# Attention, MoE and soft-MoE in one kernel: an earlier reciprocal and earlier turns of q and k in the first attention; masks, evictions and the scaling of q moved between engines in chunk 1

## The chip, the cores and the metric

The kernel runs on one core of a Trainium2 chip. The metric is device time in microseconds, lower is better. A core has TensorE (PE for its matmuls, PEld for its weight loads), VectorE (DVE), ScalarE (ACT), GpSimd (POOL) and SyncE (SP, which issues the transfers here). Each works through its own list of instructions in order, and semaphores tie the lists together.

## The reference

Three stages follow each other. `setup_inputs` scales q and k by 8 and phi by 200 and gives every input as float64; the kernel reads q, k, v and the weights as they are handed over.

```python
# 1: attention, q, k, v of shape (4, 8, 576, 64); heads 0-3 plain window 32, heads 4-7 dilated by 4
scores = scale * np.matmul(q, k.transpose(0, 1, 3, 2))
mask_plain = (rel >= 0) & (rel < window)
mask_dil = (rel >= 0) & (rel < window * dilation) & (rel % dilation == 0)
scores = np.where(masks[None, :, :, :], scores, -1000000000.0)
attn = np.exp(scores - np.max(scores, axis=-1, keepdims=True))
attn = attn / (np.sum(attn, axis=-1, keepdims=True) + 1e-09)
x = np.matmul(attn, v)                       # then (2304, 512)
# 2: h = x @ w_in (512 x 2048); x = (h - tanh(h)) @ w_out (2048 x 512)
# 3: logits = x @ phi (512 x 32); soft mixture over 8 experts of 512 -> 1024 -> 512, 4 slots each
d = np.exp(logits - logits.max(0)); d /= d.sum(0) + 1e-9; slot_input = d.T @ x
slot_out[e] = np.maximum(slot_input[e] @ w1[e], 0.0) @ w2[e]
c = np.exp(logits - logits.max(1)); c /= c.sum(1) + 1e-9; out = c @ slot_out
```

## The kernel before, in words

The 2304 tokens are worked in four chunks of 512 (one batch each) and a rest of 256. While the tokens of one chunk go through `w_in`, the attention of the next batch is computed between the matmuls. Batch 0 has nothing to run beside, so its attention stands at the front (the first attention); then comes chunk 0 of the matmuls, `mixed_step` s = 0 to 7, with the attention of batch 1 in it (the change's words call that attention "chunk 1", by its batch; this text says the mixed chunk for the eight steps). `phase_step` does the later chunks, and the experts end the kernel.

**One unit of attention.** A batch has four pairs of heads, taken in the order `PO = (2, 3, 0, 1)`, and twelve units, three for each pair. A unit goes through: `emit_scores` (8 or 6 small matmul groups on PE into a PSUM tile `mm`, L359), a row maximum on DVE (L374), exponentials on ACT (L377), a reciprocal of the sums on DVE (L391), a multiplication by it on POOL (L392), transposes on PE (L401), their eviction by ACT (`ENGS['pt']`, L103), products with v on PE (L422), and evictions of the result as a rounded high part by ACT (`xhi`) and a low part by DVE (`xlo`, L458). For batch 0 the mask is added by one more matmul (L337: a bf16 identity times a bf16 mask opens the sum in PSUM, `by_pe`), for the others DVE adds it (L371) and the exponentials read the SBUF copy.

**q and k.** For batch 0, `emit_qk` turns k (n = 0) and q (n = 1) of a pair by PE transposes (L308); k is evicted by DVE (L103), q by ACT with the factor 0.125 (L316). For later batches POOL scales q (`scale_q`, L250) and DVE turns both in blocks (`turn_qk`, L260 and L261).

**The weights.** They arrive as 64-bit words and are put together as float32: `conv_a` on ACT (L507, the high word), `conv_b` on DVE (a shift of a word, L515, and a shift with an or, L516: the word shifts). For `w_in`, `conv_in_c` casts a high part (`wh`, L103) and subtracts a low part on POOL (L529). For `w_out`, `conv_out_c` transposes the block on PE (L537) and evicts the turned words by the engine in `ENGS['wt'][ft % 2]`, so before by ACT for even blocks and by DVE for odd ones; `conv_out_d` writes the block back to DRAM and multiplies by phi on PE (L548).

**What sets the order.** In the front every step is put on a list by `at(t, ...)` with a nominal time, and the list is sorted; the times order the instructions of every engine and do nothing else. The units have `ATT0 = (8.71, 3.45)` (start and pitch); in pitches after its start a unit has its reciprocal at `NORM`, transposes at `TRANS`, products with v at `PV`; q and k of the next pair come at `QK`; blocks of `w_in` begin at `WI`, with `conv_b` at `CB` and `conv_in_c` at `IC` pitches after. `warm` fills PE with matmuls whose result is not used (L205). `mixed_step` and `phase_step` are written out in order. SP's queue follows the same program: each transfer waits there for its buffer, in order. PSUM has five `mm` buffers in turn and two `h` buffers.

**One mixed step s.** It has the h matmuls of blocks 2s and 2s + 1 (12 each: L574, L575, L576), tanh on ACT (L580), a subtraction on DVE (L583), `conv_a` to `conv_in_c` of the `w_in` blocks 2s + 2 and 2s + 3, `conv_out_c` to `conv_out_d` of the `w_out` blocks 2s + 4 and 2s + 5, `conv_a` and `conv_b` of the next two, scores of two units (2s, 2s + 1), transposes and v products of the two units before, and at s = 0, 1, 2, 4 (`QKS`) a `turn_qk`.

Of the kernel before, what the change touches and what calls it, by code (L numbers as in the profile page):

```python
# [13 lines left out]
ACTF = mybir.ActivationFunctionType  # L14
ALU = mybir.AluOpType
# [13 lines left out]
UNITS = 16  # L29
KA = 6  # L30
CAL = 2.29
MASKPE = 1
PO = (2, 3, 0, 1)
VB = (1, 2, 3)
EA = (1,)
# [1 line left out]
    ("out", 0): 0, ("out", 2): 1, ("out", 4): 2, ("in", 0): 3, ("in", 2): 0, ("in", 4): 1, ("out", 6): 2, ("in", 6): 3,  # L37
    ("out", 8): 2, ("out", 10): 1, ("in", 8): 2, ("in", 10): 3, ("out", 14): 2, ("in", 14): 3,
}
ENGS = {'qk': 'VVAA', 'pt': 'AAA', 'hi': 'AAA', 'rem': 'VVA', 'wh': 'VA', 'wt': 'AV', 'wq': 'V', 'wp': 'A'}  # L40
WARM = 5
NWARM = 4
WAT = 0.29
ATT0 = (8.71, 3.45)
NORM = (1.01, 0.28)
TRANS = [2.05] * 10 + [1.9, 1.3]
PV = [3.15] * 9 + [2.95, 2.5, 1.9]
QK = (1.54, 1.08)
LQK = (12.33, 21.85)
LV = (4.31, 7.03)  # L50
DT0 = 5.58
# [3 lines left out]
CB = 0.96  # L55
OC = 1.64
OD = 3.09
OE = 3.85
WI = (45.0, 4.0)
LWI = 2.97  # L60
IC = 0.34

# [2 lines left out]
def moe_kernel(ctx: ExitStack, tc: tile.TileContext, q, k, v, w_in, w_out, phi, w1, w2, out):  # L65
    nc = tc.nc
# [34 lines left out]
    def copy(eng, out, in_):  # L101

        (nc.scalar.copy if eng == "A" else nc.vector.tensor_copy)(out=out, in_=in_)  # L103
# [10 lines left out]
    def cpart(*dims):  # L114
        o = moff[0]
        moff[0] += size(dims)
        return view(mem[:, o:o + size(dims)], dims)
# [38 lines left out]
    wp = cpart(NFT, NS)  # L156
# [90 lines left out]

    def scale_q(b, p):
        t = raws[b, p]
        nc.gpsimd.tensor_scalar(out=t[:, 0], in0=t[:, 0], scalar1=0.125, scalar2=None, op0=ALU.mult)  # L250

    def turn_qk(b, p):

# [34 lines left out]
    def emit_qk(b, p, n):  # L288
# [16 lines left out]
        for th in range(2):  # L305
# [4 lines left out]
            if p >= NP // 2:  # L310
                ps = ps.rearrange("p e (h x) -> p e h x", h=2)
            eng = ENGS["qk"][2 * n + th]
            if n == 0:
# [12 lines left out]
    def emit_scores(b, *units):  # L326

        work = []
        for i in units:
# [3 lines left out]
            mask = mask_d[:, (0, 4, 2)[u]:(4, 8, 6)[u]] if nb == 4 else mask_p[:, min(u, 1):min(u, 1) + 3]  # L333
            by_pe = b < MASKPE
            nr = nq if by_pe else 64
# [59 lines left out]
    def emit_trans(b, i):  # L395
# [6 lines left out]
        pt = pts.next()[0:nk, 0:nb * P].rearrange("p (c k) -> p c k", c=nb)  # L402
        copy(ENGS["pt"][min(b, 2)], pt, ps)
        sc_pt[b, i] = pt

    def emit_pv(b, i):
# [44 lines left out]
        for src, f in pieces:  # L451
            copy(ENGS["hi"][min(b, 2)], f(hi), src)

        def low():
            for src, dst in rems:
                copy(ENGS["rem"][min(b, 2)], dst, src)
            for src, f in pieces:
# [62 lines left out]
    def win(part, ft):  # L520
        return wts[ft // 2][:, part, :, 128 * (ft % 2):128 * (ft % 2) + 128]

    def conv_in_c(ft):
# [3 lines left out]
        hi, lo = win(0, ft), win(1, ft)  # L527
        copy(ENGS["wh"][ft > 1], hi, fv)
        nc.gpsimd.tensor_tensor(out=lo, in0=fv, in1=hi.bitcast(F32), op=ALU.subtract)  # L529
# [3 lines left out]
    def conv_out_c(ft):  # L533
# [4 lines left out]
        wt = convs["wt"].next()  # L538
        copy(ENGS["wt"][ft % 2], wt, ps)
        wstate["wt", ft] = wt  # L540
# [26 lines left out]
    def emit_h(xh, xl, ft, ps=None, part=range(KT)):  # L567

        if ps is None:
            ps = ps_h.tile([128, 512], F32, tag="h", name="h")[:, 0:xh.shape[-1]]  # L570
        for n in part:
            kt = PO[n]
            wh, wl = win(0, ft)[:, kt, :], win(1, ft)[:, kt, :]
            nc.tensor.matmul(ps, lhsT=wh, rhs=xh[:, kt, :], start=(n == 0), stop=False)  # L574
            nc.tensor.matmul(ps, lhsT=wh, rhs=xl[:, kt, :], start=False, stop=False)  # L575
            nc.tensor.matmul(ps, lhsT=wl, rhs=xh[:, kt, :], start=False, stop=(n == KT - 1))  # L576
        return ps
# [301 lines left out]
    with tc.manual_schedule():  # L879
# [4 lines left out]
        def at(t, f, *args):  # L884
            steps.append((t, len(steps), f, args))

        for b, (t0, dt) in enumerate((ATT0,)):
            for i in range(NU):
                t = t0 + dt * i
                at(t - 0.01, emit_lows)  # L890
                at(t, emit_scores, b, i)
                at(t + NORM[b] * dt, emit_norm, b, i)
                at(t + TRANS[i] * dt, emit_trans, b, i)
                at(t + PV[i] * dt, emit_pv, b, i)
                if b == 0:
                    at(t + WAT * dt, warm, WARM if i < NWARM else 2)
            for i in (NU, NU + 0.55, NU + 0.95):
                at(t0 + dt * i, emit_lows)
            for p in range(NP):
                for n in range(2):  # L900
                    at(t0 - 0.02 + 0.01 * n if p == 0 else t0 + dt * (3 * p - 3 + n + QK[b]), emit_qk, b, PO[p], n)
                at(t0 + dt * 3 * p - LQK[b], load_qk, b, PO[p])
                at(t0 + dt * 3 * p - LV[b], load_v, b, PO[p], nc.sync)
# [4 lines left out]
        for e in range(KA):  # L908
            t, dt = WO1[0] + WO1[1] * e, WO1[1]
# [6 lines left out]
        for e in range(4):  # L916
            t, dt = WI[0] + WI[1] * e, WI[1]
            at(t - LWI if e < 2 else 45.0, load_w, "in", e)
            at(t, conv_a, "in", e)
            at(t + CB, conv_b, "in", e)  # L920
            at(t + IC * dt, conv_in_c, e)
        first = []
        for i in range(2):

            at(ATT0[0] + ATT0[1] * (12.6 + 0.4 * i), lambda i: first.append(emit_h(xhi[0], xlo[0], i, part=range(3))), i)
        at(WI[0] + 6.0, scale_q, 1, PO[0])
        for _, _, f, args in sorted(steps, key=lambda s: s[0:2]):
            f(*args)
        emit_lows()
# [14 lines left out]
        def mixed_step(an, ch, s, xh, xl, gs, posts):  # L944
# [47 lines left out]
            if s + 1 in QKS:  # L992
                scale_q(an.b, PO[QKS.index(s + 1)])
# [4 lines left out]
        def phase_step(an, ch, s, xh, xl, gs, posts):  # L998
# [29 lines left out]
            if an and s + 1 in QKS:  # L1028
                scale_q(an.b, PO[QKS.index(s + 1)])
# [133 lines left out]
        for a, copy in enumerate((nc.scalar.copy, nc.vector.tensor_copy)):  # L1163
            ps = mm([128, 2, 32])
            for c in range(2):
                dt = 2 * a + c
# [32 lines left out]
        for cols in halves:  # L1199
# [4 lines left out]
                out=sS[64:96, cols], in0=ps[64:96], in1=sS[64:96, cols].bitcast(F32), op=ALU.subtract  # L1204
# [49 lines left out]
```

## Time and profile before

| | |
|---|---|
| median of three runs (lowest to highest) | 460.63 us (460.35 to 463.51) |
| the profiled execution | 460.01 us, span 458.2 us |
| mean granted TensorE clock | 0.973 of full |
| busy share of the span | PE 92%, PEld 67%, DVE 58%, ACT 44%, POOL 18% |

The profile's shares are averages over stages that have different limits. The first attention ends at about 61 us, the mixed chunk runs to about 146 us, and from there on PE is nearly always busy. A wait of an engine is told with what released it: `[2.32 <-DVE qk L261]` reads as 2.32 us of idle time which DVE's line 261 ended. [...]

### The profile page before, as it was taken

How to read it: one execution, taken by the hardware profiler on the slowest of the kernel's cores; microseconds unless marked ns; L12 is line 12 of the kernel's file. 1: busy time of each engine (PE TensorE's matmuls, PEld its weight loads, DVE VectorE, ACT ScalarE, POOL GpSimd, SP SyncE). 2: the span in 40 equal slices, each digit the busy share in tenths (PEclk: the TensorE clock that was granted, in tenths of full speed). 3: DMA queues.
4: the chain of work that ended last, by engine and by line, in shares of the span. 5: the costliest groups of instructions: out<-in, count | busy, mean ns of one | idle time of the engine just before them, and what ended most of it. 6: DMA issues, size and time to landing. Idle time of an engine off the chain costs nothing.

```text
span 458.2 us, 11352 instructions
## 1 busy us (share of the span) xinstructions
PE 420.3 (92%) x4555; PEld 306.5 (67%) x4555; DVE 264.6 (58%) x625; ACT 200.1 (44%) x693; POOL 83.5 (18%) x99
## 2 busy tenths in 40 slices
PE   6988688898999999999999999999999999999980
PEld 4766466666777776877775777776777689555330
DVE  2666549979897667765576777444544331332051
ACT  3766438667577173655153564331211223213141
POOL 3231423424224231313031211000000000010000
PEclk9999789899899999999999999999999999999996
DMA  8999974879667303243503212094003599899938
GB/s 242 238 222 280 281 127 145 268 149 277 229 177 127 75 1 54 61 69 54 121 20 54 41 40 94 1 362 191 0 1 109 186 407 409 313 405 408 408 121 313
DMA packets 102021, 81.16 MB, mean 177 GB/s; under 512 B 78032, under 2 KB 81872, under 8 KB 101968
## 3 DMA queue, kind: packets, MB, share of 16 engines
q1 hardware_dynamic: 101968, 80.43, 58.2%
q8 instruction: 36, 0.59, 0.6%
q14 instruction: 17, 0.14, 0.1%
HBM read 71.50 MB, written 8.91 MB: 175 GB/s over the span
## 4 chain that ended last, share of the span: by engine, by line
PE 68%; DVE 14%; ACT 7%; DMA 4%; issue 2%; SPq 2%; POOL 1%; DVEq 0%; POOLq 0%; ACTq 0%
PE h L574 12%; PE h L576 11%; PE h L575 11%; PE mm L713 4%; PE lg L589 4%; ACT mem L377 3%; PE mm L359 3%; PE h L797 3%; PE mm L422 3%; PE y L822 3%; PE mm L401 3%; PE warm L205 2%; SPq L243 2%; DMA wo<-wo_dram 1%; DVE cva L516 1%
## 5 line engine op out<-in xcount | busy, mean ns | idle before, releaser
L574 PE MATMUL h<-xhi,wts 128*128 128x512 f32 x256 | 107.0, 418 | 0.0
L576 PE MATMUL h<-xhi,wts 128*128 128x512 f32 x256 | 101.4, 396 | 0.5 <-POOL wts L529 0.5
L575 PE MATMUL h<-xlo,wts 128*128 128x512 f32 x256 | 101.6, 397 | 0.0
L580 ACT ACTIVATE mem<-h 128x512 f32<-128x512 f32 x72 | 43.0, 599 | 120.1 <-PE h L576 112.6
L583 DVE TENSOR_TENSOR mem<-h,mem 128x512 f32<-128x512 f32 x72 | 49.0, 681 | 68.5 <-ACT mem L580 68.5
L392 POOL TENSOR_TENSOR mem<-mem 128x320 f32<-128x320 f32 (+1 forms) x48 | 32.9, 695 | 156.2 <-DVE mem L391 92.9
L574 PEld LDWEIGHTS h<-xhi,wts 128*128 128x128 f32 x256 | 49.4, 193 | 15.9 <-issue 5.5
L576 PEld LDWEIGHTS h<-xhi,wts 128*128 128x128 f32 x256 | 48.9, 191 | 12.1 <-POOL wts L529 0.9
L575 PEld LDWEIGHTS h<-xlo,wts 128*128 128x128 f32 x256 | 49.2, 192 | 8.8
L377 ACT ACTIVATE mem<-mem 128x80 f32<-128x80 f32 (+1 forms) x126 | 44.5, 355 | 17.0 <-DVE mem L374 17.0
L596 DVE STREAM_TRANSPOSE gt<-mem 128x512 f32<-128x512 f32 x64 | 40.9, 681 | 0.0
L103 ACT COPY mem<-mm 80x448 f32<-80x448 f32 (+4 forms) x64 | 25.5, 430 | 9.0 <-PE mm L401 7.8
L359 PE MATMUL mm<-qk 64*64 64x96 f32 (+2 forms) x672 | 23.5, 246 | 5.0 <-ACT qk L316 2.6
L422 PE MATMUL mm<-mem,v 80*64 80x48 f32 (+1 forms) x672 | 26.8, 229 | 1.0 <-ACT mem L103 1.0
L401 PE MATMUL mm<-mem 112*80 112x112 f32 (+1 forms) x168 | 23.8, 275 | 4.2 <-POOL mem L392 4.2
L589 PE MATMUL lg<-mem 128*32 128x128 f32 x576 | 25.9, 279 | 0.9 <-DVE mem L583 0.9
L422 PEld LDWEIGHTS mm<-mem,v 80*64 80x64 f32 (+1 forms) x672 | 22.8, 140 | 5.5 <-ACT mem L103 1.7
L359 PEld LDWEIGHTS mm<-qk 64*64 64x64 f32 (+1 forms) x672 | 18.0, 133 | 10.9 <-issue 4.7
L377 ACT ACTIVATION_READ_ACCUMULATOR mem<-mem 128x1 f32 x126 | 23.6, 187 | 0.0
L401 PEld LDWEIGHTS mm<-mem 112*80 112x80 f32 (+1 forms) x168 | 16.6, 124 | 9.6 <-POOL mem L392 5.5
L589 PEld LDWEIGHTS lg<-mem 128*32 128x32 f32 x576 | 14.9, 109 | 11.6 <-issue 9.0
L377 ACT ACTIVATE mem<-mm,mem 128x80 f32<-128x80 f32 (+1 forms) x42 | 13.5, 331 | 15.6 <-DVE mem L389 9.6
(178 smaller groups left out, 634.2 us busy)
## 6 DMA issues: line engine op xcount, KB each, us to landing
ex<-in_moe_w_dram SPq DMA_DIRECT2D x21, 1024.0 KB, 10.7
gt<-in_moe_w_out_dram SPq DMA_DIRECT2D x7, 1024.0 KB, 8.1
gt<-in_moe_w_in_dram SPq DMA_DIRECT2D x7, 1024.0 KB, 8.3
gt<-in_moe_w_dram SPq DMA_DIRECT2D x6, 1024.0 KB, 9.8
mem<-in_moe_w_dram SPq DMA_DIRECT2D x5, 1024.0 KB, 7.1
wo_dram<-cva SPq DMA_DIRECT2D x16, 256.0 KB, 6.0
wo<-wo_dram SPq DMA_DIRECT2D x4, 1024.0 KB, 7.5
out_dram<-o SPq DMA_DIRECT2D x8, 512.0 KB, 4.8
```

The costliest lines, as they stand in the source:

```text
L359: nc.tensor.matmul(ps[64 * y:64 * y + nr, c, :], lhsT=qT[b, p][r, q0:q0 + step * (nr - 1) + 1:step], rhs=kT[b, p][r, k0:k0 + step * (nk - ...
L377: nc.scalar.activation(out=pr[:, c, :], in_=ps[:, c, :], func=ACTF.Exp, bias=nm[:, c:c + 1], accum_out=sm[:, c:c + 1],)
L392: nc.gpsimd.tensor_tensor(out=pr, in0=pr, in1=rc.unsqueeze(2).to_broadcast([128, nb, nk]), op=ALU.mult)
L401: nc.tensor.transpose(ps[:, c, :], pr[0:P, c, :], ident[0:P, 0:P])
L422: nc.tensor.matmul(o[64 * hh:64 * hh + 64, col:col + nq], lhsT=vt[b, p](n, hh), rhs=pt[:, c, 64 * (x ^ sw):64 * (x ^ sw) + nq], start=True ...
L574: nc.tensor.matmul(ps, lhsT=wh, rhs=xh[:, kt, :], start=(n == 0), stop=False)
L575: nc.tensor.matmul(ps, lhsT=wh, rhs=xl[:, kt, :], start=False, stop=False)
L576: nc.tensor.matmul(ps, lhsT=wl, rhs=xh[:, kt, :], start=False, stop=(n == KT - 1))
L580: nc.scalar.activation(out=g, in_=ps, func=ACTF.Tanh)
L583: nc.vector.tensor_tensor(out=g, in0=ps, in1=g, op=ALU.subtract)
L589: nc.tensor.matmul(lgs[ch][32 * j:32 * j + 32, 0:128], lhsT=wp[:, ft, :], rhs=g[:, 128 * j:128 * j + 128], start=(ft == 0), stop=(ft == NF ...
L596: nc.vector.transpose(out=gt[:, ft, :], in_=g)
```

## The change

It changes numbers that order the front, two settings that choose an engine, and one function.

- `NORM`: the reciprocal of the last unit of the first attention stands at 0.6 of a pitch in place of 1.01; `WI`, and the times of `conv_b` and `conv_in_c` of the first four `w_in` blocks, are set anew.
- `QK` for batch 0: 0.75 in place of 1.54, so k and q of a pair are turned one unit sooner.
- `MASKPE = 2`: the masks of batch 1 are added by PE too (12 more matmuls), and the 12 additions on DVE go.
- `ENGS['wt'] = 'AA'`: turned words of odd `w_out` blocks are evicted by ACT as well (three in the first attention, five in the mixed chunk).
- `scale_q`: ACT scales q of batch 1, in place of POOL; the first of these stands at 56.0 on the list in place of 51.0.

```diff
-MASKPE = 1
+MASKPE = 2
-ENGS = {'qk': 'VVAA', 'pt': 'AAA', 'hi': 'AAA', 'rem': 'VVA', 'wh': 'VA', 'wt': 'AV', 'wq': 'V', 'wp': 'A'}
+ENGS = {'qk': 'VVAA', 'pt': 'AAA', 'hi': 'AAA', 'rem': 'VVA', 'wh': 'VA', 'wt': 'AA', 'wq': 'V', 'wp': 'A'}
-NORM = (1.01, 0.28)
+NORM = [1.01] * 11 + [0.6]
-QK = (1.54, 1.08)
+QK = (0.75, 1.08)
-WI = (45.0, 4.0)
+WI = (43.5, 4.0)
     def scale_q(b, p):
         t = raws[b, p]
-        nc.gpsimd.tensor_scalar(out=t[:, 0], in0=t[:, 0], scalar1=0.125, scalar2=None, op0=ALU.mult)
+        if b in EA:
+            nc.scalar.activation(out=t[:, 0], in_=t[:, 0], func=ACTF.Copy, scale=0.125)
+        else:
+            nc.gpsimd.tensor_scalar(out=t[:, 0], in0=t[:, 0], scalar1=0.125, scalar2=None, op0=ALU.mult)
...
-                at(t + NORM[b] * dt, emit_norm, b, i)
+                at(t + NORM[i] * dt, emit_norm, b, i)
...
             at(t, conv_a, "in", e)
-            at(t + CB, conv_b, "in", e)
-            at(t + IC * dt, conv_in_c, e)
+            at(t + 3.3, conv_b, "in", e)
+            at(t + (5.4 if e < 2 else 3.4), conv_in_c, e)
...
-        at(WI[0] + 6.0, scale_q, 1, PO[0])
+        at(56.0, scale_q, 1, PO[0])
```

The new lines in `scale_q` move what follows down by three lines: L359 before is L362 in the changed kernel.

DVE at the end of the first attention, before, from the maximum of unit 10 to the reciprocal of unit 10. L374 is a unit's maximum, L389 and L391 its reciprocal, L515 and L516 the word shifts (`cvb` is `w_in` block 0, `mem` block 1):

```order
L374 TENSOR_REDUCE mem<-mm 128x3
L389 TENSOR_SCALAR mem<-mem 128x3
L391 RECIPROCAL mem<-mem 128x3
L515 TENSOR_SCALAR cvb<-cvb 128x512
L516 SCALAR_TENSOR_TENSOR cvb<-gt,cvb 128x512
L103 CAST wts<-cvb 128x4x128
L103 COPY mem<-mm 128x16
L458 TENSOR_TENSOR xlo<-mm,xhi 128x3x48
L458 TENSOR_TENSOR xlo<-mm,xhi 128x32
L374 TENSOR_REDUCE mem<-mm 128x3
L389 TENSOR_SCALAR mem<-mem 128x3
L391 RECIPROCAL mem<-mem 128x3
```

The second L374 is that of unit 11, which thus stands behind the word shifts and the cast of block 0. Six rows further on (two copies, the word shifts of block 1 and the subtractions, L458) DVE comes to the last reciprocal, that of unit 11. The same stretch in the changed kernel, from the maximum of unit 11:

```order
L377 TENSOR_REDUCE mem<-mm 128x3
L392 TENSOR_SCALAR mem<-mem 128x3
L394 RECIPROCAL mem<-mem 128x3
L518 TENSOR_SCALAR cvb<-cvb 128x512
L519 SCALAR_TENSOR_TENSOR cvb<-gt,cvb 128x512
L103 COPY cvb<-mm 128x128
L392 TENSOR_SCALAR mem<-mem 128x3
L394 RECIPROCAL mem<-mem 128x3
L103 CAST wts<-cvb 128x4x128
```

The maximum of unit 11 and the reciprocal of unit 10 now stand ahead of the word shifts of block 0, and the last reciprocal ahead of those of block 1 and of the cast.

PE in the first attention, before, around the scores of unit 3, the first of the second pair. L308 turns q of that pair, L359 are the scores that need it:

```order
L205 MATMUL warm<-mem 128x256
L308 MATMUL mm<-mem,rqk 128x96 x6
L337 LDWEIGHTS mem
L337 MATMUL mm<-mem 128x320
L359 MATMUL mm<-qk 48x80 x8
L401 MATMUL mm<-mem 80x112 x4
```

In the changed kernel the same turn (L311) stands ahead of the scores of unit 2, and a whole unit with its warm-up lies between it and the scores of unit 3:

```order
L205 MATMUL warm<-mem 128x256
L311 MATMUL mm<-mem,rqk 128x96 x6
L340 LDWEIGHTS mem
L340 MATMUL mm<-mem 128x320
L362 MATMUL mm<-qk 48x80 x8
L404 MATMUL mm<-mem 80x112 x4
```

Both turns of each of the three later pairs move by one unit like that.

ACT in mixed step 1 of the changed kernel. L583 is the tanh of an h block, L510 `conv_a`, L380 the exponentials, `cvb<-mm 128x512` the evictions of turned words:

```order
L583 ACTIVATE mem<-h 128x512
L510 ACTIVATE cvb<-gt 128x512
L510 ACTIVATE mem<-gt 128x512
L103 COPY cvb<-mm 128x512 x2
L583 ACTIVATE mem<-h 128x512
L103 COPY mem<-mm 80x448 x2
L103 CAST wts<-cvb 128x4x128
L103 CAST wts<-mem 128x4x128
L510 ACTIVATE cva<-gt 128x512 x2
L380 ACTIVATE mem<-mm,mem 128x80 x4
L385 ACTIVATE mem<-mem 128x4
L251 ACTIVATE rqk<-rqk 128x576
```

Before, the list had one eviction there, exponentials that read SBUF (`mem<-mem`), and no scaling (L251) at its end. SP's list is the same in both kernels.

## Rows read from the trace of the kernel before

**Rows 1.** Windows: length, busy us (count) PE, PEld, DVE, ACT, POOL, PEclk, DMA, GB/s.

```profile
51.50:61.20 9.70, 8.61 (x48) 7.03 (x49) 3.52 (x13) 3.06 (x9) 3.54 (x3) 0.50 0.83 218
70.30:144.20 73.90, 66.80 (x728) 52.38 (x725) 67.06 (x143) 51.48 (x175) 25.74 (x25) 0.95 0.71 201
108.40:123.80 15.40, 13.12 (x134) 10.33 (x131) 14.01 (x29) 8.90 (x29) 5.95 (x6) 0.89 0.85 252
123.80:134.90 11.10, 10.22 (x120) 7.88 (x118) 10.66 (x26) 8.80 (x29) 3.50 (x5) 1.00 0.50 157
```

**Rows 2.** Waits of PE, 8 to 48 us: total us, times, longest us.

```profile
PE mm L359 <- ACT qk L316: 2.6, 3, 1.4
```

**Rows 3.** Timeline, 40 to 70 us: start, us, engine, line, operation [idle before <- releaser].

```profile
43.67 0.53 PE L401 MATMUL mm<-mem 128*96 128x128 f32 x3
51.51 0.88 PE L401 MATMUL mm<-mem 128*96 128x128 f32 x3 [3.10 <-POOL mem L392]
55.35 0.87 PE L401 MATMUL mm<-mem 128*96 128x128 f32 x3 [1.08 <-POOL mem L392]
...
69.53 0.82 PE L359 MATMUL mm<-qk 64*64 64x80 f32 x32 [2.32 <-DVE qk L261]
```

**Rows 4.** Timeline of PE and of DVE, first attention: a mask matmul, a maximum from PSUM.

```profile
10.23 0.31 PE L337 MATMUL mm<-mem 64*128 64x320 bf16 x1
...
8.25 0.49 DVE L374 TENSOR_REDUCE mem<-mm 128x4 f32<-128x320 f32 x1 [2.22 <-PE mm L359]
```

**Rows 5.** Groups by form, 70.28 to 144.18 us: count, busy us, mean ns, idle before.

```profile
L515 DVE TENSOR_SCALAR cva<-cva 128x512 uint32<-128x512 uint32 x10 | 5.8, 575 | 0.0
L250 POOL TENSOR_SCALAR rqk<-rqk 128x576 f32<-128x576 f32 x3 | 5.3, 1765 | 0.0
L507 ACT ACTIVATE cvb<-gt 128x512 f32<-128x512 f32 x5 | 3.4, 683 | 0.0
L103 DVE COPY cvb<-mm 128x512 f32<-128x512 f32 x5 | 3.4, 671 | 0.0
L103 ACT COPY cvb<-mm 128x512 f32<-128x512 f32 x5 | 3.0, 601 | 0.0
L374 DVE TENSOR_REDUCE mem<-mem 128x4 f32<-128x320 f32 x6 | 2.9, 486 | 0.2
L371 DVE TENSOR_TENSOR mem<-mm,mem 128x320 f32<-128x320 f32 x6 | 2.9, 480 | 0.0
L515 DVE TENSOR_SCALAR cvb<-cvb 128x512 uint32<-128x512 uint32 x6 | 2.4, 402 | 0.0
```

**Rows 6.** Waits of PE and of ACT, 70 to 146 us: total, times, longest.

```profile
PE mm L537 <- DVE cva L516: 5.4, 7, 1.5
...
ACT mem L580 <- PE h L576: 8.7, 4, 3.7
```

**Rows 7.** Transfers: SP's issues, us to landing of two, ACT's first use of each.

```profile
68.00 0.48 SPq L241 DMA_DIRECT2D rqk<-in_k_dram  x1
74.58 0.39 SPq L486 DMA_DIRECT2D gt<-in_moe_w_out_dram  x1
gt<-in_moe_w_out_dram SPq DMA_DIRECT2D x1, 1024.0 KB, 5.3
82.98 1.23 ACT L507 ACTIVATE cva<-gt 128x512 f32<-128x512 f32 x2
87.33 0.38 SPq L482 DMA_DIRECT2D gt<-in_moe_w_in_dram  x1
100.87 0.45 SPq L486 DMA_DIRECT2D raww<-in_moe_w_out_dram  x1
raww<-in_moe_w_out_dram SPq DMA_DIRECT2D x1, 1024.0 KB, 8.0
110.56 1.23 ACT L507 ACTIVATE cva<-raww 128x512 f32<-128x512 f32 x2
```

**Rows 8.** Waits of PE, 146 to 458 us, the longest in total.

```profile
PE mm L713 <- ACT mem L677: 1.1, 2, 0.6
```

## Prediction, before the changed kernel was run

> **What bounds the kernel now.** I read the windows first, then PE's waits, then the timelines at the places where PE stands still, then the transfers. PE is the engine to follow: in the steady chunks it is nearly always busy, and behind 146 us its longest wait in total is 1.1 us [rows 8], so whatever the front and the mixed chunk win or lose reaches the end in full. The loss lies ahead of 146 us, at four kinds of places. In the first attention PE waits three times, 2.6 us in all, for ACT's eviction of q, always just ahead of a pair's first scores [rows 2]. [...] At the door of the mixed chunk PE waits 2.32 us until DVE has turned q and k [rows 3]. In the mixed chunk (73.9 us) DVE is busy for 67.06 us and PE for 66.80 [rows 1]: PE waits seven times, 5.4 us in all, for word shifts [rows 6], and the step from 108.4 us, where the clock averages 0.89, lasts 15.4 us against 11.1 us for the next one at 1.00 [rows 1].
>
> **The first attention: turns one unit sooner.** Two turns for each of three pairs move past one unit's matmuls and warm-up on PE; nothing is added. No wait for ACT was longer than 1.4 us [rows 2], and a whole unit now covers it. The raw q and k are there: SP's list is the same, and PE had no wait for them at these places. Gain 2.6 us; at the low end 1.5, if three more evictions of turned words on ACT (0.60 us each [rows 5]) push the exponentials.
>
> **Its end: the reciprocals.** DVE now takes the maximum of unit 11 and the reciprocal of unit 10 ahead of the word shifts of block 0, and the last reciprocal ahead of the cast and of block 1. Both gaps, 3.10 and 1.08 us, should close. With them goes the reason for the slow clock: three transposes take 0.53 us at full clock and 0.88 behind the gap [rows 3], a ratio of 0.60, so 8.61 us of busy PE would be 5.2, 3.4 us less. Together 7.6 us. What comes next there is new: the cast of block 1 now stands behind a copy that waits for a product on PE, and POOL's subtraction for block 1 follows the cast, so the h matmuls of block 1 may wait. The nearest size is the second gap, 1.08; I leave 1.2 us of waiting there. This part gives 6.4 us; at the low end 3.0, if the clock falls all the same.
>
> **The door of the mixed chunk.** The turn on DVE still ends the wait, but the list ahead of it has lost an eviction (0.67 us [rows 5]), and two mask matmuls (at most 0.31 us each [rows 4]) fill part of the rest. The scaling of q was off the path and stays so. Of 2.32 us I count 1.0 as won, between 0 and 2.3. Sum at the chunk's first scores: 2.6 + 6.4 + 1.0 = 10.0 us earlier.
>
> **The mixed chunk.** DVE loses twelve mask additions (0.48 us, 5.8 us at most) and five evictions (3.4 us); the word shifts that ran beside POOL's scaling get shorter: the cva shifts average 575 ns, the cvb ones 402, so up to 1.7 us over ten [rows 5]. PE gains twelve masks, at most 3.7 us [rows 4]. ACT gains five evictions of 0.60 us and three scalings; no row has a scaling there, so between 0.68 (512 columns from SBUF to SBUF on ACT) and 1.77 us (the same on POOL) [rows 5], and I take 0.75, since 576 columns on the same engine are nearest to the first. That is 5.3 us over the chunk, about 1.35 in a step that has both; ACT waits for PE 8.7 us in four waits ahead of a tanh, 2.2 us each [rows 6], and this hides it. The maximum now reads PSUM: 0.49 us against 0.486 from SBUF [rows 4, 5], so it costs nothing. [...]
>
> With some 10 us less on DVE, PE would set the chunk. But **transfers** come in. SP runs without a pause until its last transfer of q and k is issued at 68.48 us; the next weights (block 8 of `w_out`) went out at 74.58, landed 5.3 us later, and ACT used them at 82.98 [rows 7]. With everything 10 us earlier they are wanted at 73.0. SP's stream starts about 1 us earlier (it hangs on blocks written back in the first attention), so it can issue them at 67.5, and they land at 72.8: just in time, and nothing is won in step 1. The second bottleneck of this kind runs from the issue at 87.33, when a buffer comes free, to block 12, issued at 100.87 and landed 8.0 us later at 108.87, used at 110.56 [rows 7]: steps 2 and 3 can win only 1.7 us unless the stream gets denser; I take 1.0. Step 4 (15.4 us) is no longer held: its stall and its slow clock go, and it comes to some 12.4 us, the 11.1 of the next step [rows 1] with 1.3 for the turn and the masks. Gain 3.0. In steps 5 to 7 the masks cost what DVE gives back; I take a loss of 0.5. The chunk: 1.0 + 3.0 - 0.5 = 3.5 us.
>
> **The sum.** 10.0 + 3.5 = 13.5 us, from the 460.0 us of the profiled execution to 446.5. The median of the runs lies 0.6 us above the profiled one, so I forecast a median of **447 us**.
>
> **Rivals.**
> - *PE sets the chunk.* The transfers keep up. Of 73.9 us PE was idle for 7.1; a mean clock of 0.95 means 7.4 us at the lower level, of which 40%, 3.0 us, would go; the masks cost 3.7 [rows 1, 4]. The chunk wins 6.4 us, and if the 1.2 us left at block 1 go too, 17.6 in all: 443 us. For it: DVE's relief is larger than the gap to PE. Against: the two streams of transfers. Chance 0.15.
> - *The transfers set the chunk.* If SP's stream is not earlier at all and block 8 takes 8.0 us, as block 12 did, it lands at 76.5, 6.5 us before its old use [rows 7]. Then only 6.5 of the 10 us survive, and the chunk wins nothing: 454 us. For it: SP has no pause ahead of 68.48. Against: the 5.3 us that block 8 took. Chance 0.18.
> - *The clock falls anyway* at the end of the first attention, because several short waits stand where one long one stood: 3.4 us less, 450.5 us. Chance 0.08.
> - *Slower: ACT becomes the bound.* Its place is the mixed step, where two evictions now stand ahead of the second tanh; the next h matmuls need that tanh's `h` buffer. It decides from the point where the added 1.35 us exceed the 2.2 us that ACT waits for PE there. If everything added lay on the path (8 evictions of 0.60 us, 3 scalings of 0.75, 3.7 us of masks: 10.8 us), and the same ACT list held up the last unit's exponentials so that the gap and its slow clock stayed, only 2.6 us would stand against it: 469 us. Against: ACT is busy for 51.5 of 73.9 us [rows 1]. Chance 0.04.
>
> The forecast itself has 0.55. The range 441 to 453.5 takes in the low and high ends of the unknown sizes and most of the second rival; some 0.07 lie below and 0.13 above. A change of 1%, 4.6 us, is about the least that can be told from none here. Faster by more, below 456.0 us: 0.92; within: 0.05; slower: 0.03.
>
> **What the new profile would show.** Right: no wait of PE for ACT's q at L362; no wait of 3 us at the last transposes, and a granted clock near 1.00 between 45 and 60 us; first scores of batch 1 at about 59.5 us; no wait of DVE's list on POOL's scaling; a step 4 of some 12 us at full clock. The step on transfers is right if ACT or DVE waits for a DMA at block 8 near 73 us. Wrong: a clock of 0.5 behind 48 us, PE waiting for tanh or for an exponential (a `mm` buffer is now held until ACT has read the scores), or a mixed chunk longer than 74 us.

## The result and the profile after

The changed kernel takes 447.94 us (median of four runs, 447.38 to 451.02) against 460.95 us for the kernel before on the same chip: a ratio of 0.972, 95% interval 0.966 to 0.978. The profiled execution took 448.4 us with a span of 446.5, 11.7 us under the span before. Executions of one kernel lie some 2 us and more apart together with their mean granted clock (in y2 445.62 us at 0.992 and 447.70 at 0.987), so differences of 1 us between versions are read from the traces, and one run of y3 (452.55 us, 1.6% above its fastest) is left out of that kernel's median.

The windows of the changed kernel (columns as in [rows 1]): the end of the first attention, the mixed chunk, its steps 4 and 5.

```profile
50.00:60.00 10.00, 8.96 (x74) 6.48 (x75) 6.55 (x15) 4.09 (x10) 3.91 (x4) 1.00 0.83 251
62.90:132.50 69.60, 64.88 (x740) 50.24 (x740) 59.69 (x128) 54.50 (x184) 21.29 (x23) 1.00 0.88 232
99.00:111.40 12.40, 11.55 (x136) 8.96 (x135) 11.36 (x24) 9.67 (x31) 3.97 (x5) 1.00 1.05 314
111.40:123.00 11.60, 10.34 (x118) 7.79 (x118) 10.51 (x25) 9.03 (x30) 3.56 (x5) 1.00 0.62 189
```

The stretch at half clock (0.50) of [rows 1] is gone, the first window above shows 1.00; step 4 lasts 12.4 us in place of 15.4, at 1.00 in place of 0.89. In the chunk DVE's work fell by 7.4 us and ACT's grew by 3.0; PE is idle for 4.7 us of 69.6, before for 7.1 of 73.9.

PE's waits between 8 and 150 us, the same kernel (total us, times, longest):

```profile
PE mm L540 <- DVE cva L519: 3.2, 6, 0.8
PE mm L362 <- DVE qk L264: 1.2, 1, 1.2
PE mm L311 <- ACT mem L380: 1.1, 2, 0.8
PE h L579 <- POOL wts L532: 1.0, 2, 0.6
PE mm L404 <- POOL mem L395: 0.9, 2, 0.6
...
```

The wait for ACT's q [rows 2] is no longer in the list. In its place stands one that was not there: the turn of q or k (L311) waits for exponentials (L380), 1.1 us. A wait of PE for an exponential was one of the prediction's signs of being wrong. The two gaps of 3.10 and 1.08 us [rows 3] have shrunk to 0.9 in all, the wait for word shifts from 5.4 us [rows 6] to 3.2. The places, from PE's timeline:

```profile
48.23 0.53 PE L404 MATMUL mm<-mem 128*96 128x128 f32 x3 [0.58 <-POOL mem L395]
...
50.17 0.53 PE L404 MATMUL mm<-mem 128*96 128x128 f32 x3 [0.32 <-POOL mem L395]
...
55.39 0.50 PE L577 MATMUL h<-xhi,wts 128*128 128x512 f32 x1 [0.25 <-DVE wts L103]
...
56.74 0.50 PE L579 MATMUL h<-xhi,wts 128*128 128x512 f32 x1 [0.62 <-POOL wts L532]
...
62.12 0.80 PE L362 MATMUL mm<-qk 64*48 64x80 f32 x32 [1.19 <-DVE qk L264]
```

The last row is the door of the mixed chunk: first scores of batch 1 at 62.12 us, 7.4 us earlier than before. They had been forecast at about 59.5.

Since the executions reach unit 3 up to 1.2 us apart (at 15.92 us in x6, at 17.11 in x5), the kernels are compared by intervals between starts of rows on PE: from the scores of unit 3 (the first of the second pair) to those of unit 11 (the last), from there to the first h matmul, from there to the first scores of batch 1, and steps 1 to 6 of the mixed chunk, from the logits of step 0 to those of step 6 (L589 before, L592 after; step 7 takes 7.0 us before and 6.9 after). Each number is the difference of two starts, in us; the names are those of the experiments below.

| kernel | unit 3 to 11 | 11 to h | h to scores | chunk | median of runs (lowest) |
|---|---|---|---|---|---|
| before | 29.18 | 12.70 | 10.99 | 73.90 | 460.95 |
| changed | 28.31 | 6.86 | 10.18 | 69.59 | 447.94 (447.38) |
| x1: turns back | 29.19 | 7.34 | 10.21 | 69.20 | 450.05 (448.57) |
| x8: k's turns back | 27.34 | 6.87 | 10.19 | 69.16 | 447.34 (446.06) |
| x4: last reciprocal back | 28.31 | 9.92 | 11.66 | 69.00 | 451.58 (451.05) |
| x2: end back | 28.31 | 12.01 | 11.93 | 69.01 | 454.86 (454.10) |
| x3: chunk's edits back | 27.62 | 7.33 | 10.52 | 72.40 | 451.69 (451.28) |
| x5: masks on DVE | 28.30 | 6.87 | 10.27 | 70.77 | 448.63 (447.08) |
| x6: evictions on DVE | 27.63 | 7.33 | 10.18 | 71.34 | 449.80 (448.01) |
| x7: scaling on POOL | 28.30 | 6.87 | 10.52 | 68.40 | 447.38 (446.44) |
| x9: load later | 28.29 | 6.87 | 10.18 | 70.46 | 449.12 (447.57) |
| y1: x8 and x7 | 27.34 | 6.87 | 10.53 | 70.04 | 446.80 (445.55) |
| y2: y1, three evictions | 26.69 | 7.34 | 10.53 | 68.60 | 446.66 (445.36) |
| y3: y2, one scaling | 26.68 | 7.34 | 10.20 | 68.61 | 447.23 (445.30) |

The table also shows how far single traces carry. x1, x8, x4 and x2 leave the list of the chunk as it is in the changed kernel, and their chunks are 69.0 to 69.2 us long, its own 69.6. So a difference of less than some 0.6 us in the chunk is not told from none.

### The profile page after: what moved, and what is told of

Same layout as the page of the kernel before. It is cut to its first block, busy times and chain, and to the rows that moved or that the text cites. A ratio compares the mean times of both kernels' runs of the same rounds, so it can differ in the third digit from the quotient of the medians.

```text
span 446.5 us, 11368 instructions
## 1 busy us (share of the span) xinstructions
PE 415.9 (93%) x4567; PEld 302.1 (68%) x4567; DVE 254.0 (57%) x605; ACT 204.0 (46%) x705; POOL 77.2 (17%) x95
## 4 chain that ended last, share of the span: by engine, by line
PE 60%; issue 13%; DVE 9%; ACT 7%; DMA 4%; SPq 3%; POOL 1%; ACTq 0%; POOLq 0%; DVEq 0%
PE h L577 10%; PE h L579 9%; PE h L578 9%; PE lg L592 3%; PE h L800 3%; PE y L825 3%; PE mm L362 3%; ACT mem L380 3%; PE mm L716 3%; SPq L243 3%; PE mm L404 3%; PE mm L425 3%; DMA wo_dram<-cva 3%; PE warm L205 2%; PE mm L311 1%
## 5 line engine op out<-in xcount | busy, mean ns | idle before, releaser
L577 PE MATMUL h<-xhi,wts 128*128 128x512 f32 x256 | 105.2, 411 | 0.2 <-DVE wts L103 0.2
L579 PE MATMUL h<-xhi,wts 128*128 128x512 f32 x256 | 100.2, 392 | 1.0 <-POOL wts L532 1.0
L578 PE MATMUL h<-xlo,wts 128*128 128x512 f32 x256 | 100.0, 391 | 0.0
L583 ACT ACTIVATE mem<-h 128x512 f32<-128x512 f32 x72 | 42.9, 597 | 115.3 <-PE h L579 107.8
L577 PEld LDWEIGHTS h<-xhi,wts 128*128 128x128 f32 x256 | 48.2, 188 | 15.7 <-issue 6.1
L579 PEld LDWEIGHTS h<-xhi,wts 128*128 128x128 f32 x256 | 48.1, 188 | 12.6 <-POOL wts L532 1.9
L578 PEld LDWEIGHTS h<-xlo,wts 128*128 128x128 f32 x256 | 48.2, 188 | 8.5
L380 ACT ACTIVATE mem<-mem 128x80 f32<-128x80 f32 (+1 forms) x84 | 29.7, 355 | 15.8 <-DVE mem L377 15.8
L380 ACT ACTIVATE mem<-mm,mem 128x80 f32<-128x80 f32 (+1 forms) x84 | 26.6, 329 | 12.5 <-DVE mem L392 7.9
L592 PE MATMUL lg<-mem 128*32 128x128 f32 x576 | 25.9, 279 | 0.9 <-DVE mem L586 0.9
L362 PE MATMUL mm<-qk 64*64 64x96 f32 (+2 forms) x672 | 23.2, 245 | 1.2 <-DVE qk L264 1.2
L362 PEld LDWEIGHTS mm<-qk 64*64 64x64 f32 (+1 forms) x672 | 17.7, 131 | 7.6 <-issue 3.8
L592 PEld LDWEIGHTS lg<-mem 128*32 128x32 f32 x576 | 14.9, 109 | 11.7 <-issue 9.0
L461 DVE TENSOR_TENSOR xlo<-mm,xhi 128x144 fp32r<-128x144 f32 (+4 forms) x72 | 16.0, 266 | 7.2 <-ACT xhi L103 7.2
```

Source lines behind the costliest of these rows:

```text
L362: nc.tensor.matmul(ps[64 * y:64 * y + nr, c, :], lhsT=qT[b, p][r, q0:q0 + step * (nr - 1) + 1:step], rhs=kT[b, p][r, k0:k0 + step * (nk - ...
L380: nc.scalar.activation(out=pr[:, c, :], in_=ps[:, c, :], func=ACTF.Exp, bias=nm[:, c:c + 1], accum_out=sm[:, c:c + 1],)
L583: nc.scalar.activation(out=g, in_=ps, func=ACTF.Tanh)
L592: nc.tensor.matmul(lgs[ch][32 * j:32 * j + 32, 0:128], lhsT=wp[:, ft, :], rhs=g[:, 128 * j:128 * j + 128], start=(ft == 0), stop=(ft == NF ...
```

## The experiments

**x1, both turns back at their old place.**

```diff
-QK = (0.75, 1.08)
+QK = (1.54, 1.08)
```

> The changed kernel with one number put back: both turns (of q and of k) of the first attention's pairs stand one unit later again, as in the kernel before; the end of the first attention and the mixed chunk stay changed. Theory (what the two traces suggest): the earlier turns took away 2.6 us of waits for ACT's q, but DVE then copied the turned k ahead of the word shifts and of a maximum, so exponentials came late and PE waited for a score buffer instead; net gain 0.8 us. So with the turns back the first scores of batch 1 come about 0.8 us later than in the changed kernel (62.9 instead of 62.1 us), the waits for ACT's q are back (2 to 2.6 us in all) and the waits of the score matmuls for the exponentials in the first attention are gone; time about 448.7 us. Rival (the prediction's own term): the turns are worth 2.6 us, and something else in the front lost 1.8: first scores at 64.7 us, time 450.5. Second rival: the turns are worth nothing: 447.9.

Ratio to before 0.976 (0.972 to 0.979). PE's waits between 8 and 48 us in x1:

```profile
PE mm L362 <- ACT qk L319: 2.7, 3, 1.4
PE mm L540 <- DVE qk L103: 0.5, 1, 0.5
```

The waits for q are back in full, those of L311 gone. Yet unit 3 to 11 grew by 0.9 us, not 2.6; another 0.5 us fell on the gaps at the last transposes, and the first scores came at 63.67 us, between the theory's 62.9 and the rival's 64.7. The mechanism is the theory's; its 0.8 us is 1.4 with those gaps. The median, 2.1 us above the changed kernel's, lies nearer to the rival's 450.5; the lowest runs lie 1.2 us apart.

**x8, only k back.**

```diff
-at(t0 - 0.02 + 0.01 * n if p == 0 else t0 + dt * (3*p - 3 + n + QK[b]), emit_qk, b, PO[p], n)
+at(t0 - 0.02 + 0.01 * n if p == 0 else t0 + dt * (3*p - 3 + (1.54 if n == 0 else 1.75)), emit_qk, b, PO[p], n)
```

> The changed kernel with q's turns one unit sooner, as in it, but k's turns left at the place of the kernel before. Theory: the 0.8 us instead of 2.6 us that the sooner turns won come from k: its two copies on DVE (1.2 us together) stand ahead of a maximum. With k back, ACT's q is still in time (no wait for ACT's q of over 0.5 us in the first attention), the score matmuls no longer wait 0.84 us for an exponential, and the time is 1 to 1.8 us below the changed kernel: 446.1 to 446.9 us. Rival (the copies of k cost PE the same at any place, since DVE is full in the first attention): the scores wait for DVE's k instead, and the time is that of the changed kernel, 447.9 us, or up to 1 us above it.

Ratio 0.970 (0.966 to 0.974). The changed kernel first, the timeline around unit 4, whose scores end on PE at about 21.2 us:

```profile
20.13 1.18 DVE L103 COPY qk<-mm 128x288 f32<-128x288 f32 x2 [1.77 <-PE mm L311]
...
20.50 0.76 PE L362 MATMUL mm<-qk 64*48 64x80 f32 x16
...
21.15 0.42 DVE L518 TENSOR_SCALAR cva<-cva 128x512 uint32<-128x512 uint32 x1
21.60 0.69 DVE L519 SCALAR_TENSOR_TENSOR cva<-gt,cva 128x512 uint32<-128x512 uint32 x1
...
22.47 0.48 DVE L377 TENSOR_REDUCE mem<-mm 128x4 f32<-128x320 f32 x1
...
23.05 0.33 ACT L380 ACTIVATE mem<-mm,mem 128x80 f32<-128x80 f32 x1 [2.92 <-DVE mem L392]
...
24.44 0.47 PE L311 MATMUL mm<-mem,rqk 96*128 96x96 f32 x3 [0.84 <-ACT mem L380]
```

The copies of k push the word shifts, these push the maximum, ACT stands idle for 2.92 us until it can start the exponentials, and PE's next turn waits for these: the exponentials read the `mm` buffers that the turns also write. The same unit in x8:

```profile
19.56 0.76 PE L362 MATMUL mm<-qk 64*48 64x80 f32 x16
...
20.36 0.49 DVE L377 TENSOR_REDUCE mem<-mm 128x4 f32<-128x320 f32 x1 [0.29 <-PE mm L362]
...
20.95 0.33 ACT L380 ACTIVATE mem<-mm,mem 128x80 f32<-128x80 f32 x1 [1.26 <-DVE mem L392]
...
22.26 1.23 DVE L103 COPY qk<-mm 128x288 f32<-128x288 f32 x2 [0.50 <-PE mm L311]
```

The maximum starts 0.80 us after the scores do, in place of 1.97; no turn waits for exponentials, and unit 3 to 11 is 0.97 us shorter. The theory's 1 us in the trace; of the runs' medians 0.6, of the lowest 1.3.

**x4, the last reciprocal behind the cast of block 0 and the subtractions.**

```diff
-NORM = [1.01] * 11 + [0.6]
+NORM = [1.01] * 12
```

> The changed kernel with the last unit's reciprocal alone put back behind the cast and the subtractions of block 0 on DVE (still ahead of the shifts of block 1). Theory: what mattered was that word shifts of two blocks stood ahead of the two last reciprocals; with the reciprocal behind one cast and its subtractions only, PE waits up to 1 us more at the last transposes, the clock stays at 1.00, and the time is 0 to 1 us above the changed kernel's: 448 to 449 us. Rival: the last reciprocal is what closes the gap that drops the clock: with it back a gap of 2 us or more opens at the last transposes, the clock goes to 0.5 behind it, and the time is 451.5 to 453.5 us.

Ratio 0.979 (0.975 to 0.982). The theory fell and the rival holds, with a gap just under its 2 us. PE's timeline and the windows of x4:

```profile
47.56 0.53 PE L404 MATMUL mm<-mem 128*96 128x128 f32 x3 [0.58 <-DMA v<-in_v_dram]
...
51.13 0.88 PE L404 MATMUL mm<-mem 128*96 128x128 f32 x3 [1.96 <-POOL mem L395]
...
54.33 0.80 PE L577 MATMUL h<-xhi,wts 128*128 128x512 f32 x1
```

```profile
47.50:50.00 2.50, 1.62 (x19) 1.13 (x19) 2.11 (x8) 2.30 (x7) 1.28 (x2) 1.00 0.94 263
...
52.50:55.00 2.50, 2.50 (x19) 2.22 (x20) 0.16 (x2) 1.27 (x5) 0.00 (x0) 0.50 0.98 344
55.00:57.50 2.50, 2.50 (x8) 1.93 (x7) 0.33 (x3) 0.00 (x0) 0.00 (x0) 0.50 1.03 240
57.50:60.00 2.50, 2.23 (x25) 1.09 (x23) 1.27 (x5) 0.28 (x1) 0.73 (x1) 0.99 0.36 55
```

The gap at the last transposes is 1.96 us in place of 0.32, 1.64 more. But the first scores of batch 1 come 4.5 us later after unit 11's (the table's 3.06 and 1.48): behind the gap PE is busy throughout at 0.50 (52.5 to 57.5 us), and an h matmul shows 0.80 us in place of 0.50. What comes behind the gap costs nearly twice what the gap does.

**x2, the whole end back.**

```diff
-NORM = [1.01] * 11 + [0.6]
+NORM = [1.01] * 12
-WI = (43.5, 4.0)
+WI = (45.0, 4.0)
-            at(t + 3.3, conv_b, "in", e)
-            at(t + (5.4 if e < 2 else 3.4), conv_in_c, e)
+            at(t + CB, conv_b, "in", e)
+            at(t + IC * dt, conv_in_c, e)
-        at(56.0, scale_q, 1, PO[0])
+        at(WI[0] + 6.0, scale_q, 1, PO[0])
```

> The changed kernel with the end of the first attention as before: the last reciprocal behind the cast, the casts, subtractions and shifts of w_in 0 and 1 and the scaling of q at their old places in the order. The sooner turns, the masks by TensorE, ACT's evictions and ACT's scaling stay. Theory: the order of DVE's list at the end of the first attention is the largest single part: the two gaps of PE (3.1 and 1.1 us) come back, and the granted clock behind the first of them is near 0.5 for some 9 us; first scores of batch 1 some 5.8 us later (67.9 us). The steps behind it keep their lengths, so the time is 447.9 + 5.8 = 453.7 us. Rival 1 (transfers take part): the work starts later but the transfers do not, so block 8 is there in time and up to 2 us of the later start are won back in the first two steps of the mixed chunk: 451.7 us. Rival 2 (the gaps close but the clock's part of 3.4 us was something else): 451 us with a clock near 1.00 behind 48 us.

Ratio 0.985 (0.982 to 0.988), 6.9 us above the changed kernel: more than theory and rivals. PE's timeline, and a window behind the second gap:

```profile
50.12 0.53 PE L404 MATMUL mm<-mem 128*96 128x128 f32 x3 [2.63 <-POOL mem L395]
...
53.74 0.88 PE L404 MATMUL mm<-mem 128*96 128x128 f32 x3 [2.00 <-POOL mem L395]
...
68.87 1.32 PE L362 MATMUL mm<-qk 64*48 64x80 f32 x32 [1.85 <-DVE qk L264]
```

```profile
57.50:60.00 2.50, 2.50 (x7) 1.99 (x6) 0.44 (x3) 0.49 (x1) 0.00 (x0) 0.50 0.57 86
```

Both gaps and the half clock are back. The transposes behind the first gap still take 0.53 us, as at full clock; those behind the second take 0.88. Besides, the door's wait is 1.85 us. From unit 11 to the first scores that is 5.15 + 1.75 = 6.9 us, and the logits come another 0.5 later behind them, since the scores run at a slower clock too (1.32 us in place of 0.80; the mean clock is 0.89 between 65 and 70 us). The end of the first attention is the greatest part of the change.

**x3, only the front of the change.**

```diff
-MASKPE = 2
+MASKPE = 1
-ENGS = {..., 'wt': 'AA', ...}
+ENGS = {..., 'wt': 'AV', ...}
-        if b in EA:
+        if b in ():
```

> The changed kernel with the three edits of the mixed chunk taken back (masks added by DVE, the second eviction of turned words in each block on DVE, q scaled by POOL); the first attention's new order stays. Theory: the front's win of 7.4 us at the first scores of batch 1 stays as it is or grows by up to 1 us (ACT has three evictions less in the first attention), and what the mixed chunk itself won, 4.3 us, is lost: 447.9 + 4.3 = 452.2 us. Rival 1 (the transfers limit the chunk, so that an earlier start is given back in it): step 1 grows by 2 us or more and the time is 454 us or more. Rival 2 (the chunk gained because its matmuls start at a full clock and better placed, not by relieving DVE): the chunk stays as short as in the changed kernel and the time is 448 us.

Ratio 0.980 (0.977 to 0.983). Steps 1, 2 and 4 of the chunk in x3:

```profile
63.10:74.60 11.50, 11.50 (x132) 9.22 (x128) 11.29 (x24) 8.03 (x28) 3.80 (x4) 0.86 0.98 219
74.60:88.40 13.80, 11.94 (x152) 9.25 (x148) 13.46 (x26) 9.57 (x32) 6.06 (x6) 1.00 0.87 265
...
99.80:115.20 15.40, 13.08 (x134) 10.28 (x131) 14.02 (x29) 8.85 (x29) 5.96 (x6) 0.89 0.94 274
```

Step 4 is as long and as slow as in the kernel before [rows 1], so its gain is due to the chunk's edits. In all they are worth 2.8 of the chunk's 4.3 us. The other 1.5 come without them: step 2 took 15.8 us at a mean clock of 0.89 before and takes 13.8 at 1.00 here, while step 1 is 0.7 longer than before, at 0.86. Neither rival holds. The theory's time, 452.2 us, is 0.5 above the median, but its sum did not come: the chunk lost 2.8 us and not 4.3.

**x5, the masks on DVE (`MASKPE = 1` alone).**

> The changed kernel with the masks of batch 1 added by DVE again (twelve additions of 0.48 us) and not by TensorE; all else stays. Theory (DVE's list is what PE waits for in the mixed chunk): the chunk grows by some 2 to 3 us of the 5.8 us that come back to DVE, since PE loses twelve masks of at most 0.31 us at the same time: 450 to 451 us. Rival (PE sets the chunk): the masks on PE cost what they save, and with them on DVE the time stays or falls by up to 1.5 us: 446.4 to 447.9 us.

Ratio 0.973 (0.970 to 0.976). The chunk is 1.2 us longer; steps 1 and 4 grow, step 2 shrinks. The theory has the sign, with about half of its size; the medians (0.7 us apart, with overlapping intervals) do not part it from no change.

**x6, the second eviction on DVE (`'wt': 'AV'` alone).**

> The changed kernel with the second eviction of turned words of each block on DVE again (eight of 0.67 us on DVE in place of 0.60 us on ACT, three of them in the first attention). Theory: the wait of PE for DVE's shifts and turns grows by about the five evictions that return to the mixed chunk, part of them hidden: 1 to 2.5 us more, 449 to 450.4 us. Rival (ACT is the engine short of time, in the first attention above all): the exponentials come sooner, and the time falls by up to 1 us: 447 us.

Ratio 0.976 (0.972 to 0.980). Both hold, each at its place: the chunk grows by 1.75 us, step 4 alone by 2.0 at a mean clock of 0.88, and unit 3 to 11 shrinks by 0.7. But the gaps at the last transposes grow by 0.5, as x6's waits between 8 and 62 us show:

```profile
PE mm L404 <- POOL mem L395: 1.4, 2, 1.1
```

**x7, q scaled by POOL.**

```diff
-        if b in EA:
+        if b in ():
```

> The changed kernel with q of batch 1 scaled by POOL again (three multiplications of 1.77 us) and not by ACT. Theory: the scaling is off the path, but it stands beside DVE's word shifts and ahead of POOL's subtractions; the shifts beside it are longer, by up to 1.7 us in all, and DVE no longer waits 2.8 us for ACT's scaling: time 447.5 to 449.5 us. Rival (a DVE that shares with POOL is the cause of the chunk's gain): step 4 has its wait for word shifts of over 2 us again, a granted clock under 0.95, and the time is 450.5 us or more.

Ratio 0.972 (0.968 to 0.976). The chunk is 1.2 us *shorter* (0.6 to 0.8 against the other kernels with its list), which neither expected, though the medians (0.6 us apart) do not part it from no change; the rival's slow step 4 did not come (12.7 us at 1.00). What the changed kernel has and x7 does not, from DVE's waits between 60 and 150 us in the changed kernel:

```profile
DVE qk L264 <- ACT rqk L251: 2.8, 3, 1.6
```

The scaling itself is short on ACT (0.70 us against 1.77 on POOL [rows 5]), but it stands at the end of ACT's list in its step, and DVE's turn waits for it. That this wait is what PE loses by is argued, not shown: DVE waits 0.8, 1.6 and 0.4 us in steps 1, 2 and 4, while x7 is 0.4, 0.7 and 0.5 us shorter in steps 2, 3 and 5, equal in step 1 and 0.3 longer in step 4. At the door it is the other way round: with POOL PE waits 1.53 us there, with ACT 1.19.

**x9, block 8 ahead of a pair's q and k in SP's list.** `an.load(3, 2)` fetches q and k of the third pair; the expectation calls it the last, whose transfers stay where they are. The transfer that the prediction has issued at 68.48 us as the last of q and k is the third pair's too.

```diff
-            an.load(*{0: (3, 2), 2: (4, 3), 3: (4, 4)}.get(s, (0, 0)))
+            an.load(*{0: (2, 2), 1: (3, 2), 2: (4, 3), 3: (4, 4)}.get(s, (0, 0)))
```

> The changed kernel with the transfers of the last pair's q and k issued one step later in the mixed chunk, so that block 8 of w_out and the next block of w_in stand ahead of them in SP's list and land sooner. Theory (the prediction's step on transfers): ACT waits 0.49 us for block 8, and step 1 and 2 are held by it; with it sooner the first two steps of the chunk (10.5 and 13.7 us) are 0.5 to 1.5 us shorter: 446.4 to 447.4 us. Rival (the transfers are not what holds the chunk: ACT's wait for block 8 lies beside other work): the steps keep their lengths and the time stays at 447.9 us, or the last pair's q and k come late and it grows by up to 2 us.

Ratio 0.975 (0.971 to 0.980). ACT's wait for block 8 is gone, and step 1 is as long as it was, 10.54 us: that wait did not hold the chunk, as the rival has it. Step 2 is 0.5 us shorter, no more than in x1, x8 and x4, where the transfers stayed. Steps 3 to 5 together are 1.4 longer: DVE now waits 1.3 us for the pair's k, and ACT 1.4 us for block 12, so transfers can hold the chunk when they are moved. The changed kernel's own wait for block 8, which the prediction named, is this (SP's issue, ACT's use):

```profile
69.73 0.81 SPq L489 DMA_DIRECT2D gt<-in_moe_w_out_dram  x1
...
75.56 0.66 ACT L510 ACTIVATE cva<-gt 128x512 f32<-128x512 f32 x1 [0.49 <-DMA gt<-in_moe_w_out_dram]
```

x4 and x2 say the same of a later start: with 4.5 and 7.4 us more from unit 11 to the chunk's logits their chunks are only 0.6 us shorter, and x8's, which starts no later, is 0.4 shorter too. In x2 step 1 is 0.9 us longer, at a mean clock of 0.90, and its other steps together are 1.45 shorter; more than that the transfers cannot be worth there.

**y1, y2 and y3: the better parts together.** y1 joins x8 and x7. y2 has the first attention's three evictions on DVE besides; y3 is y2 with the scaling ahead of the chunk on ACT.

```diff
-        copy(ENGS["wt"][ft % 2], wt, ps)
+        copy("V" if ft in (1, 3, 5) else "A", wt, ps)
-        if b in ():
+        if b in EA and p == PO[0]:
```

> The changed kernel with two parts taken back that the runs showed to be worth less than nothing: k's turns at the old place (q's stay one unit sooner), and q of batch 1 scaled by POOL again. Theory: the two lie in different stages and add up. From unit 3's scores to unit 11's k's old place was worth 1.0 us (28.3 to 27.3 us), and in the mixed chunk the scaling on POOL 1.2 us (69.6 to 68.4 us); 447.9 - 2.2 = 445.7 us. Rival (both relieve DVE at the same place, the turn of the first pair at the chunk's door, or an earlier front is given back to transfers in the chunk's first steps): only the larger part stays, 446.7 us or more.

> As the version with k's turns back and q scaled by POOL, and three of the eight evictions that went to ACT, those of the first attention, on DVE again; the five of the mixed chunk stay on ACT. Theory: in the first attention ACT's three evictions cost PE 0.46 us between the scores of unit 9 and of unit 11 (6.44 us against 5.98 with them on DVE), in the mixed chunk they are worth 1.75 us; with each where it is cheaper the time is 0.5 us below the version without this: 445.2 us. Rival (with k's turns back DVE has no room at that place, or the last reciprocals come later behind the eviction and the two gaps at the last transposes grow from 0.9 to 1.4 us, as they do with all eight on DVE): no change or up to 0.3 us slower: 445.7 to 446.0 us.

> As the version with k's turns back, q scaled by POOL and the first attention's three evictions on DVE, but the first pair's q, the one that is scaled ahead of the mixed chunk, is scaled by ACT again; POOL scales the three in the chunk. Theory: with the first scaling on POOL PE waited 1.5 us for DVE's turn at the chunk's door, with it on ACT 1.2 us; so the first scores come 0.3 us sooner and the time is 0.3 us below that version's lowest run of 445.4 us; and if the slow clock that some profiled executions show behind the door comes with the longer wait, the median falls towards the lowest run: 445.1 to 446.0 us. Rival (the door's wait comes from the list ahead of the turn on DVE, not from the scaling, and the slow stretches fall where they will): door 1.5 us, median 446.7 us.

Ratios 0.970 (0.967 to 0.974), 0.971 (0.966 to 0.976) and 0.969 (0.965 to 0.974). In the traces of y2 and y3 the parts add up: unit 3 to 11 falls from 28.3 to 26.7 us, the chunk to 68.6, y3's door is at 1.2 us, and its span is 443.6 us, 2.9 under the changed kernel's. y1's chunk took 70.0 us in the profiled execution, for a slow stretch that the last section shows. In y2 the evictions win 0.65 us and the gaps take back 0.47, as its rival had it. The intervals of all three overlap that of the changed kernel, so that the runs do not show them to be faster; the lowest runs stand 1.8 to 2.1 us lower. y1's and y2's medians lie nearer to their rivals, their lowest runs near the theories' 445.7 and 445.2. Of y3's theory the door came; that the median would fall to the lowest run did not (447.2 against 445.3 us).

## Why the prediction was right, and where it was not

The time was right to 0.9 us, with two errors that offset each other in part: the front won 7.4 us, not 10.0, the chunk 4.3, not 3.5. Luck hid half of the miss: between the profiled executions the sum missed by 1.9 us (448.4 against 446.5), but the median, which I had put 0.6 us above the profiled time, fell 0.5 below it.

**The turns: 2.6 us forecast, 0.9 found,** below the low end of 1.5. The waits for ACT's q went, as predicted. The step that failed is "nothing is added": I followed the moved turns on PE and looked at the evictions on ACT only as a low end, but not at k's copies on DVE, which came ahead of a maximum. x8 prices them at 1.0 us, x6 the three evictions at 0.7 between unit 3 and 11. With both away (y2) this stretch is 2.5 us shorter than before, nearly the whole of the term. The 0.1 us by which unit 3 starts later than before is less than executions differ there.

**The end: 6.4 us forecast, 5.5 found** (6.65 us from unit 11 to the first scores, less 1.13 at the door). x4 and x2 show that the order on DVE makes the gap, and that the half clock comes with it. That the gap's length alone brings it is not shown; the last section has gaps of one length with either clock. By terms: the gaps won 3.3 of 4.2 us, since 0.58 and 0.32 us are left where I had said that both should close. Of the 1.2 us I left at block 1, 0.87 came, on the engines named. The rest, PE's busy time, gives 3.1 by difference, where I had 3.4 for the clock: from the 8.61 us of busy PE at 0.50 in the first window of [rows 1], at the ratio of 0.53 to 0.88 us in [rows 3].

**The door: 1.0 forecast, 1.13 found** (2.32 to 1.19 us). That the scaling is off the path there did not hold: with POOL doing it the wait is 1.53 us (x7), so it is 0.34 of the 1.13.

**The chunk: 3.5 forecast, 4.3 found, partly for another reason.** Step 4 came out as forecast (12.4 us, 1.00), steps 2 and 3 won 1.7 us where I had 1.0, step 1 0.3 where I had none, the steps behind step 4 lost 0.7 where I had 0.5. But the transfers, by which I held steps 1 to 3 back, are worth little: SP issued block 8 at 69.73 us, later than the 67.5 I had, and still ACT waited only 0.49 us for it, a wait that could go without shortening step 1 (x9). That wait was my sign that the step on transfers is right; it came, and the step was wrong. What took part of DVE's relief was ACT's scaling. I hid it behind ACT's waits for PE; those waits stand ahead of a tanh, the scaling is at the end of the step, and DVE's turns waited for it. Undoing it is worth 0.6 to 1.2 us of the chunk (x7); the way from DVE's wait to PE is argued. Nor did the word shifts get shorter: L515 and L518 took 14.3 us before and 14.1 after, and not 1.7 less. The shifts of `cva` beside the scaling had indeed been long (0.56 to 0.80 us), but in the changed kernel three others took 1.06 to 1.07 us, each beside one of POOL's subtractions (L532), which the change leaves in place; the rest took 0.4 to 0.5.

**The maxima.** Twelve now read PSUM; the six with 320 columns average 479 ns, against 486 from SBUF [rows 5], the six with 288 columns 446, against 453. The step that it costs nothing held.

**The rivals.** That PE sets the chunk holds in part: it is busy for 64.9 of 69.6 us, yet x3 and x6 still lengthen it by work given back to DVE. The transfers, the fallen clock and the bound on ACT did not come; ACT's price was a scaling that came late, not its load (54.50 us busy of 69.6). The first rival's 7.4 us at the lower level rest on a clock of two levels; the trace before shows that: of 276 windows of half a microsecond between 8 and 146 us, 239 have 1.00, 31 have 0.50, and six lie between; in the changed kernel all 276 have 1.00.

Still open: how the 1.5 us that the chunk wins without its own edits divide between the earlier start and slow stretches that fall differently in each execution.

## What to carry to other kernels

When a step is moved, follow every instruction that it issues on every engine to what it is now ahead of; here the two copies behind a moved transpose took two fifths of the gain. Close the gap ahead of a long run of matmuls first: in x4 a gap longer by 1.64 us cost another 2.9 behind it, at the lower clock. An engine with spare time can still be the wrong place for a piece of work, if its list comes to it late: look at who waits for that piece, not at the busy share alone (ACT was busy for 54.50 us of 69.6, and DVE's turns waited 2.8 us for its scaling).

## What was not expected of the hardware

The half clock comes in some executions and not in others at one place. The timeline of PE and a window of y1 at the door, and then of y2:

```profile
60.94 0.81 PE L362 MATMUL mm<-qk 64*48 64x80 f32 x32 [1.53 <-DVE qk L264]
...
63.09 0.63 PE L579 MATMUL h<-xhi,wts 128*128 128x512 f32 x1
```

```profile
62.50:65.00 2.50, 2.50 (x7) 1.93 (x7) 2.43 (x5) 2.47 (x16) 0.67 (x1) 0.50 1.12 160
```

```profile
60.53 0.81 PE L362 MATMUL mm<-qk 64*48 64x80 f32 x32 [1.50 <-DVE qk L264]
...
62.19 0.40 PE L579 MATMUL h<-xhi,wts 128*128 128x512 f32 x1
```

```profile
62.50:65.00 2.50, 2.50 (x15) 1.98 (x13) 2.43 (x5) 2.44 (x17) 0.27 (x1) 1.00 1.44 141
```

The same list and the same wait, and the same matmul takes 0.63 or 0.40 us; y1's chunk is 1.4 us longer than y2's, all of it in step 1. Among the profiled executions, a stretch under 1.00 stood behind the door in three of the seven kernels that waited 1.5 us or more there (x2 with a wait of 1.85 us and a mean clock of 0.90 in step 1, x3 with 1.87 and 0.86, y1 as above; not x5 with 1.63, x7 with 1.53, y2 with 1.50, nor the kernel before, with the longest wait, 2.32 us), and in none of the seven that waited 1.16 to 1.19. So the length of the wait does not settle it, and what does is open. That a shorter door would steady the time was not borne out by y3's runs, which reach from 445.3 to 449.2 us.
